# The last tiles' output sums of MoE 2 in PSUM banks of their own, one for each half of the last tile

## The chip, the cores and the metric

The kernel runs on one core of a Trainium2 chip. The metric is device time of one execution in microseconds (us); less is better. The core's engines are TensorE (PE, matmuls; its weight loads are listed apart as PEld), VectorE (DVE), ScalarE (ACT), GpSimd (POOL) and SyncE (SP, which issues the DMA transfers here). Matmuls accumulate in PSUM, which the program holds as one tile `pb` of 8 banks, each 128 partitions x 512 fp32 numbers.

## The reference

Three stages follow one another; the inputs are fp32, 2 batches x 768 positions = 1536 tokens, model width 512.

```python
attn = softmax(q @ k^T / 8 + bias, only where keep) @ v        # 2 x 8 heads x 768 x 64
x = attn, heads side by side                                   # 1536 x 512

h = x @ w_in                                                   # MoE 1: 512 -> 2048
P = a[0] + a[1]*h + a[2]*h**2 + a[3]*h**3
Q = 1 + abs(b[0])*abs(h) + abs(b[1])*h**2
y = (P / (Q + 1e-6)) @ w_out                                   # 2048 -> 512

h = y @ w2_in                                                  # MoE 2: 512 -> 1024
e = exp(h - max(h)); sm = e / (sum(e) + 1e-9)                  # along the 1024
s = h * sm
ln = (s - mean(s)) / sqrt(var(s) + 1e-6) * g_ln
out = ln @ w2_out                                              # 1024 -> 512
```

## The kernel before

**Numbers.** Every fp32 operand of a matmul is split in a high part (a cast to fp32r) and a low part (the fp32 number less the high part), and each product is three matmuls: high x high, high x low, low x high. So an operand needs a cast on ACT and a subtraction on DVE or POOL (the helper `minus`, all of whose instructions have line L99). The weights come in as words that are converted first (`w_conv`: a scaled copy into a PSUM bank on ACT, L565; bit operations in that bank on DVE or POOL and DVE, a shift at L586; a join back to SBUF on DVE, L574) and then split (`w_split`: high part on ACT, L604; low part on POOL or DVE).

**MoE 1.** The tokens go in blocks of 384, the width 2048 in slices of 128. For one block and one slice, `h_mm` makes h transposed, 128 x 384, in one bank (12 matmuls: 8 with the high weights and inputs, L634 and L636, 4 with the low inputs, L640), `e_ops` makes the fraction from it in a row of steps on ACT and DVE (L660 to L675), whose result is cast by ACT (L677, tile `g`) and subtracted by POOL (L99), and `y_mm` adds the slice's share of y into three banks (6 matmuls with the high part, L725 and L726, then 3 with the low part, L731). Of the last block the y sums of its three tiles stay in banks 5, 6 and 7 until three additions on DVE (L747) carry them to SBUF.

**MoE 2.** It goes in 12 tiles of 128 tokens (`NTILE`), called tile 0 to 11 here, in six functions:
- `p2_front`: y is transposed on PE (L791, four matmuls, "yT" below), cast to `yh` by ACT (L797) and subtracted to `yl` by DVE (L99).
- `p2_h`: the first product, in two halves of 512 columns, 12 matmuls each (L810 to L812), in two banks: 2 and 3 for even tiles, 4 and 5 for odd ones ("H2a" and "H2b" are the halves of tile 2).
- `p2_soft`: maximum (DVE, L832), exponential (ACT, L857), product with h (DVE, L838), squares (ACT, L859), an inverse root (ACT, L846 and L847, one Newton step on DVE, L850 to L853) and the normalisation (DVE, L854).
- `p2_tr`: the result is transposed on PE in two halves (L872, "lT"), each in bank 0 or 1, cast to `lh` by ACT (L880) and subtracted to `ll` by DVE (L99).
- `p2_o`: the second product, 24 matmuls over 512 columns (L894 to L896, "O0" to "O11"), all tiles in bank 7, `Val("y2")`; a copy to SBUF by ACT (L903, tile `ot`); a DMA to the output from SP (L905). Tile 11 goes in two halves of 256 columns, with two copies and two DMAs; both halves lie in the same bank, and the bank is one `Val`.

**What sets the order.** The functions above don't issue instructions, they record operations by `op(engine, duration, function, r, w, new, ...)`: values read, written, newly placed. The class `Plan` gives each a due time (`deadlines`), worked backwards along the dependencies, and then runs all engines against assumed durations (`run`): at each step, of the operations that can start now on an engine, the one due first is taken. A value made with `new` needs a free place in its pool. The PSUM pools are h (banks 0, 1), s (2, 3), p (4), y0 (5), y1 (6) and y2 (7); the values of one line take their places in the order in which they were recorded, so the weight conversions, the even tiles' first products and the attention scores follow one another in banks 2 and 3. Dependencies are by value. The argument `after` adds dependencies on whole operations; these count for the order alone.

Lines that matter, of `p2_h` and `p2_o`:

```python
for half in range(2):
    op("PE", 3.06, lambda half=half: mm(half), r=[...],
       new=[o.h[half]] if half else [o.h[0]], occ=2.76, tag="h2")

b, ot = Val("y2"), Val("wst", "ot")
parts = [op("PE", 5.52 / n + 0.3, lambda c=c: mm(c), r=[...],
            **{"w" if i else "new": [b]}, occ=5.52 / n, tag="o") for i, c in enumerate(cs)]
```

## Time and profile before

| | us |
|---|---|
| median of 3 runs (lowest to highest) | 559.95 (559.59 to 560.86) |
| the profiled execution's own time | 558.11 |
| its span in the trace | 556.3 |
| PE busy over the span | 531.8 (96%) |
| DVE busy | 446.0 (80%) |
| ACT busy | 393.0 (71%) |
| POOL busy | 182.5 (33%) |

The granted clock of TensorE is 0.999 of full speed, 2.4 GHz, over the whole execution. Attention and MoE 1 are interleaved up to about 400 us; the last first product of MoE 1 on PE ends at 390.63 us, and from 413 us on PE does MoE 2 alone. The last matmul starts at 550.15 us, and the rest of the span, some 6 us, is the last copies, their DMAs and the program's end.

How it is read: the windows show which engine is full in which stretch, the waits show what PE and DVE stood idle for, and the timelines show single instructions around the two places that the change touches, the passage from MoE 1 to MoE 2 and the last tiles. In a row of a timeline the bracket at its end is the idle time of the engine ahead of it and the instruction that ended it.

### The profile page before, as it was taken

How to read it: one execution, taken by the hardware profiler on the slowest of the kernel's cores; microseconds unless marked ns; L12 is line 12 of the kernel's file. 1: busy time of each engine (PE TensorE's matmuls, PEld its weight loads, DVE VectorE, ACT ScalarE, POOL GpSimd, SP SyncE). 2: the span in 40 equal slices, each digit the busy share in tenths (PEclk: the TensorE clock that was granted, in tenths of full speed). 3: DMA queues.
4: the chain of work that ended last, by engine and by line, in shares of the span. 5: the costliest groups of instructions: out<-in, count | busy, mean ns of one | idle time of the engine just before them, and what ended most of it. 6: DMA issues, size and time to landing. Idle time of an engine off the chain costs nothing.

```text
span 556.3 us, 8937 instructions
## 1 busy us (share of the span) xinstructions
PE 531.8 (96%) x2910; PEld 437.0 (79%) x2910; DVE 446.0 (80%) x1104; ACT 393.0 (71%) x911; POOL 182.5 (33%) x212
## 2 busy tenths in 40 slices
PE   7999999999999899999999999999999999999995
PEld 6668776877788678778788887888878788888874
DVE  4997999999999999878788999999876755455530
ACT  5688999898888878787778988898544543334330
POOL 2311665546456632122342644674510000000000
PEclk9999999999999999999999999999999999999999
DMA  7469662544354432211013322252101111000011
GB/s 252 130 201 341 195 219 86 185 135 153 104 182 154 151 96 98 73 48 48 1 38 114 133 77 75 77 180 87 57 20 38 39 38 58 20 19 20 19 39 43
DMA packets 28278, 56.24 MB, mean 101 GB/s; under 512 B 3520, under 2 KB 11968, under 8 KB 28224
## 3 DMA queue, kind: packets, MB, share of 16 engines
q1 hardware_dynamic: 28080, 55.59, 30.9%
q8 instruction: 25, 0.41, 0.3%
q14 instruction: 29, 0.24, 0.1%
q10 hardware_dynamic: 144, 0.00, 0.0%
HBM read 47.72 MB, written 7.86 MB: 100 GB/s over the span
## 4 chain that ended last, share of the span: by engine, by line
PE 55%; DVE 29%; ACT 10%; issue 4%; DMA 1%; POOL 0%; SPq 0%; ACTq 0%; DVEq 0%; POOLq 0%
PE pb L894 4%; PE pb L896 4%; PE pb L895 4%; PE pb L634 4%; PE pb L810 4%; PE pb L812 4%; PE pb L811 4%; PE pb L640 4%; PE pb L731 3%; PE pb L636 3%; PE pb L725 3%; DVE t L667 3%; PE pb L459 3%; DVE wst L574 3%; PE pb L726 3%
## 5 line engine op out<-in xcount | busy, mean ns | idle before, releaser
L99 POOL TENSOR_TENSOR g<-t,g 128x384 fp32r<-128x384 f32 x64 | 69.2, 1082 | 103.9 <-ACT g L677 91.7
L634 PE MATMUL pb<-x,w 128*128 128x384 f32 x256 | 89.3, 349 | 1.8 <-DVE t L667 1.8
L636 PE MATMUL pb<-x,w 128*128 128x384 f32 x256 | 86.1, 336 | 0.0
L725 PE MATMUL pb<-w,g 128*128 128x512 f32 x192 | 77.5, 404 | 4.2 <-ACT g L677 4.2
L726 PE MATMUL pb<-w,g 128*128 128x512 f32 x192 | 75.6, 394 | 0.5 <-POOL w L99 0.5
L99 POOL TENSOR_TENSOR w<-wst,w 128x512 fp32r<-128x512 f32 x42 | 57.2, 1364 | 42.7 <-ACT w L604 38.8
L640 PE MATMUL pb<-x,w 128*128 128x384 f32 x256 | 58.0, 347 | 0.1
L731 PE MATMUL pb<-w,g 128*128 128x512 f32 x192 | 57.7, 409 | 0.2 <-POOL g L99 0.2
L634 PEld LDWEIGHTS pb<-x,w 128*128 128x128 f32 x256 | 48.1, 188 | 8.6 <-DVE t L667 4.4
L471 ACT ACTIVATE e<-e,st 128x256 f32<-128x256 f32 (+1 forms) x96 | 46.3, 486 | 6.4 <-DVE st L464 6.4
L640 PEld LDWEIGHTS pb<-x,w 128*128 128x128 f32 x256 | 44.5, 188 | 7.1 <-issue 3.1
L636 PEld LDWEIGHTS pb<-x,w 128*128 128x128 f32 x256 | 48.1, 188 | 1.5
L725 PEld LDWEIGHTS pb<-w,g 128*128 128x128 f32 x192 | 36.0, 187 | 14.4 <-ACT g L677 7.3
L660 ACT ACTIVATE t<-pb,coef 128x384 f32<-128x384 f32 x64 | 42.7, 668 | 6.1 <-PE pb L640 6.1
L482 POOL TENSOR_SCALAR e<-e,st 128x256 f32<-128x256 f32 (+1 forms) x58 | 28.0, 495 | 54.4 <-DVE st L477 48.4
L669 ACT ACTIVATE t<-t,coef 128x384 f32<-128x384 f32 x64 | 39.6, 618 | 6.8 <-DVE t L667 6.6
L662 DVE TENSOR_TENSOR t<-t,pb 128x384 f32<-128x384 f32 x64 | 35.2, 549 | 11.1 <-ACT t L663 6.5
L677 ACT CAST g<-t 128x384 fp32r<-128x384 f32 x64 | 32.8, 512 | 16.0 <-DVE t L675 15.3
L880 ACT CAST lh<-pb 128x512 fp32r<-128x512 f32 x24 | 13.9, 592 | 42.5 <-PE pb L872 42.5
L459 PE MATMUL pb<-qk 64*128 64x256 f32 (+3 forms) x192 | 41.3, 393 | 2.7 <-DVE st L464 1.0
L667 DVE SCALAR_TENSOR_TENSOR t<-pb,coef,t 128x384 f32<-128x384 f32 x64 | 39.2, 613 | 5.2 <-ACT pb L666 4.8
L671 DVE SCALAR_TENSOR_TENSOR t<-t,t 128x384 f32<-128x384 f32 x64 | 40.6, 634 | 1.3 <-ACT t L670 1.3
(113 smaller groups left out, 1293.2 us busy)
## 6 DMA issues: line engine op xcount, KB each, us to landing
wst<-in_w_in SPq DMA_DIRECT2D x24, 512.0 KB, 4.0
wst<-in_w_out SPq DMA_DIRECT2D x24, 512.0 KB, 3.7
qk<-in_qkv SPq DMA_DIRECT2D x40, 256.0 KB, 2.7
v<-in_qkv SPq DMA_DIRECT2D x40, 128.0 KB, 2.5
y_d<-y SPq DMA_DIRECT2D x12, 256.0 KB, 2.5
y<-y_d SPq DMA_DIRECT2D x12, 256.0 KB, 2.6
out<-wst SPq DMA_DIRECT2D x11, 256.0 KB, 2.0
qk<-in_qkv SPq DMA_DIRECT2D x8, 192.0 KB, 3.7
```

The costliest lines, as they stand in the source:

```text
L99: eng.tensor_tensor(out=out, in0=a, in1=hi.bitcast(F32), op=ALU.subtract)
L459: pe.matmul(out=score(h), lhsT=a[r, h * 128:(h + 1) * 128], rhs=a[r, 256:256 + w], start=True, stop=True)
L471: act.activation(out=e[:, h, 0:w], in_=e[:, h, 0:w], func=AF.Exp, scale=-1.0, bias=st[:, h:h + 1], accum_out=st[:, 2 + 2 * h:3 + 2 * h])
L634: pe.matmul(out=pb[:, g.h.slot, 0:n], lhsT=wt[wh.slot][:, cs[p]], rhs=xt[x[p][0].slot][:, 0:n], start=(p == 0), stop=False)
L636: pe.matmul(out=pb[:, g.h.slot, 0:n], lhsT=wt[wl.slot][:, cs[p]], rhs=xt[x[p][0].slot][:, 0:n], start=False, stop=False)
L640: pe.matmul(out=pb[:, g.h.slot, 0:n], lhsT=wt[wh.slot][:, cs[p]], rhs=xt[x[p][1].slot][:, 0:n], start=False, stop=(p == 3))
L660: op("ACT", 0.2 + 0.46 * k, lambda: act.activation(out=T(g.c), in_=h(), func=AF.Identity, scale=coef[:, 3:4], bias=coef[:, 2:3]), r=[g.h], ...
L667: op("DVE", 0.2 + 0.41 * k, lambda: stt_(out=T(g.a), in0=h(), scalar=coef[:, 5:6], in1=T(g.b), op0=ALU.mult, op1=ALU.add), r=[g.h, g.b], n ...
L671: op("DVE", 0.15 + 0.41 * k, lambda: stt_(out=T(g.a), in0=T(g.a), scalar=1.0 + 1e-6, in1=T(g.b), op0=ALU.add, op1=ALU.mult), r=[g.b], w=[g ...
L725: pe.matmul(out=pb[:, y[i].slot, :], lhsT=gt[g.gh.slot][:, c], rhs=wt[wh.slot], start=g.first, stop=False)
L726: pe.matmul(out=pb[:, y[i].slot, :], lhsT=gt[g.gh.slot][:, c], rhs=wt[wl.slot], start=False, stop=False)
L731: pe.matmul(out=pb[:, y[i].slot, :], lhsT=gt[g.gl.slot][:, c], rhs=wt[wh.slot], start=False, stop=g.last)
```

## The change

**In `p2_o`.** The sums of tile 10 go to bank 6 (`Val("y1")`) instead of bank 7. The halves of tile 11 are two values: the first in bank 7, the second in bank 2 (`Val("s")`); each copy reads only its own. Tiles 0 to 9 stay in bank 7.

**In `p2_h`.** The first half of a tile's first product now claims both banks of the tile at once, where each half claimed its own before. Both halves depend, through `after`, on all the conversions' scaled copies recorded so far but the last two (`scaled`, filled in `w_conv`).

The diff also brings two further switches, `ROOT` and `EARLY`, which are off (`False` and empty) and leave the program as it is, but for a small SBUF tile `cf` that nothing uses. No instruction is added or removed: each engine executes the same operations, in another order from about 298 us of the old trace on.

```diff
+ROOT, EARLY, ENDS = False, (), True
...
-    nconv, nlo = [0], [0]
+    nconv, nlo, scaled = [0], [0], []
...
-        op("ACT", 0.63, scale, r=[st], new=[bank] + list(new), lead=WLEAD, tag="wsc")
+        scaled.append(op("ACT", 0.63, scale, r=[st], new=[bank] + list(new), lead=WLEAD, tag="wsc"))
...
             op("PE", 3.06, lambda half=half: mm(half), r=[o.yh, o.yl] + [v for m in range(4) for v in W["i2", m, half]],
-               new=[o.h[half]] if half else [o.h[0]], occ=2.76, tag="h2")
+               **{"w" if half else "new": o.h[1:] if half else o.h}, occ=2.76, after=scaled[:-2], tag="h2")
...
-        b, ot = Val("y2"), Val("wst", "ot")
-
-        def mm(c):
+        ot = Val("wst", "ot")
+        bs = [Val("y2")] if n == 1 else [Val("y2"), Val("s" if ENDS else "y2")]
+        if ENDS and o.k == NTILE - 2:
+            bs = [Val("y1")]
+        if n == 2 and not ENDS:
+            bs[1] = bs[0]
+
+        def mm(c, b):
...
-        parts = [op("PE", 5.52 / n + 0.3, lambda c=c: mm(c), r=[o.lh, o.ll] + [v for f in range(8) for v in W["o2", f]],
-                    **{"w" if i else "new": [b]}, occ=5.52 / n, tag="o") for i, c in enumerate(cs)]
         for i, c in enumerate(cs):
-            op("ACT", 0.59 / n, lambda c=c: act.copy(wst[ot.slot].bitcast(F32)[:, c], pb[:, b.slot, c]), r=[b],
+            b = bs[i]
+            op("PE", 5.52 / n + 0.3, lambda c=c, b=b: mm(c, b), r=[o.lh, o.ll] + [v for f in range(8) for v in W["o2", f]],
+               **{"w" if i and b is bs[0] else "new": [b]}, occ=5.52 / n, tag="o")
+        for i, c in enumerate(cs):
+            b = bs[i]
+            op("ACT", 0.59 / n, lambda c=c, b=b: act.copy(wst[ot.slot].bitcast(F32)[:, c], pb[:, b.slot, c]), r=[b],
                **{"w" if i else "new": [ot]}, tag="ot")
```

The order moves at three places. In the rows below `L` is the line (the second file has other numbers), the tile written stands left of the arrow and the tiles read right of it; `pb` is PSUM, `w` a weight, `wst` a staging tile that also holds MoE 2's exponentials, and the number behind a name's underline only tells the buffer.

**PE where MoE 1 ends.** Before, from the last two matmuls of a y sum (high part of `g0`) on; then come the first product's first matmuls of tile 0 (`yh0`):

```order
L725 MATMUL pb_89<-w56_148,g0_169 128x512
L726 MATMUL pb_89<-w57_149,g0_169 128x512
L810 MATMUL pb_89<-w1_93,yh0_2936 128x512
L811 MATMUL pb_89<-w0_92,yh0_2936 128x512
L812 MATMUL pb_89<-w1_93,yl0_2938 128x512
```

Now, from the same two matmuls on (L725, L726 and L731 have become L767, L768 and L773; L791 is L833, L810 is L852):

```order
L767 MATMUL pb_89<-w56_148,g0_169 128x512
L768 MATMUL pb_89<-w57_149,g0_169 128x512
L833 MATMUL pb_89<-ident_65,y2_191 128x128 x4
L773 MATMUL pb_89<-w56_148,g1_170 128x512 x3
L767 MATMUL pb_89<-w58_150,g2_171 128x512
L768 MATMUL pb_89<-w59_151,g2_171 128x512
L767 MATMUL pb_89<-w58_150,g2_171 128x512
L768 MATMUL pb_89<-w59_151,g2_171 128x512
L767 MATMUL pb_89<-w58_150,g2_171 128x512
L768 MATMUL pb_89<-w59_151,g2_171 128x512
L852 MATMUL pb_89<-w1_93,yh0_2937 128x512
```

The first transpose of y and the next y sum (high part of `g2`) now stand ahead of tile 0's first product, which starts one y sum later. On ACT, correspondingly, the cast `yh0` now stands right ahead of the cast to that `g2`; before, it stood nine instructions further ahead, in front of the cast to `g0` as well. Behind these rows PE did H0b, yT1, H1a, both lT of tile 0, yT2, H1b, H2a, H2b, with three y sums among the first of them; now it does H0b, yT1, H1a, yT2, H1b, H2a, lT0a, H2b, lT0b, with the y sums all ahead of H1a.

**DVE around tile 0's normalisation.** Before, from the last Newton step on (L854 is the normalisation, L586 and L574 the last weight conversion, in bank 2, L747 the three y sums, L832 the maximum of tile 1):

```order
L853 TENSOR_SCALAR st20_2940<-st20_2940 128x1
L854 TENSOR_SCALAR wst0_156<-wst0_156,st20_2940 128x1024
L586 SCALAR_TENSOR_TENSOR pb_89<-pb_89,wst3_159 128x512
L747 TENSOR_TENSOR y1_190<-pb_89,y1_190 128x512
L747 TENSOR_TENSOR y3_192<-pb_89,y3_192 128x512
L747 TENSOR_TENSOR y0_189<-pb_89,y0_189 128x512
L574 SCALAR_TENSOR_TENSOR wst3_159<-wst3_159,pb_89 128x512
L99 TENSOR_TENSOR yl0_2938<-pb_89,yh0_2936 128x512
L99 TENSOR_TENSOR ll0_2945<-pb_89,lh0_2943 128x512
L832 TENSOR_REDUCE st21_2941<-pb_89 128x1
```

Now (L896 is the normalisation, L618 and L606 the conversion, L789 the y sums, L874 the maximum of tile 1):

```order
L789 TENSOR_TENSOR y3_192<-pb_89,y3_192 128x512
L789 TENSOR_TENSOR y0_189<-pb_89,y0_189 128x512
L789 TENSOR_TENSOR y1_190<-pb_89,y1_190 128x512
L885 TENSOR_SCALAR st20_2941<-st20_2941 128x1
L892 TENSOR_TENSOR st20_2941<-st20_2941 128x1
L893 SCALAR_TENSOR_TENSOR st20_2941<-st20_2941 128x1
L894 SCALAR_TENSOR_TENSOR st20_2941<-st20_2941 128x1
L895 TENSOR_SCALAR st20_2941<-st20_2941 128x1
L896 TENSOR_SCALAR wst0_156<-wst0_156,st20_2941 128x1024
L618 SCALAR_TENSOR_TENSOR pb_89<-pb_89,wst3_159 128x512
L103 TENSOR_TENSOR yl0_2939<-pb_89,yh0_2937 128x512
L606 SCALAR_TENSOR_TENSOR wst3_159<-wst3_159,pb_89 128x512
L874 TENSOR_REDUCE st21_2942<-pb_89 128x1
```

The y sums moved ahead of the normalisation, the low part of the third y (`yl0`) between the two steps of the conversion, and `ll0` behind the maximum of tile 1.

**PE between the last tiles' second products.** Before, from the last three matmuls of O8 to the first three of O9 (each in bank 7):

```order
L894 MATMUL pb<-w_123,lh_2943 128x512
L895 MATMUL pb<-w_122,lh_2943 128x512
L896 MATMUL pb<-w_123,ll_2945 128x512
L872 MATMUL pb<-ident,wst_156 128x128 [waits DVE_49]
L872 MATMUL pb<-ident,wst_156 128x128 x3
L894 MATMUL pb<-w_109,lh_2944 128x512 [waits Activation_49]
L895 MATMUL pb<-w_111,lh_2944 128x512
L896 MATMUL pb<-w_109,ll_2946 128x512
```

Now, the same two products, each still in bank 7:

```order
L941 MATMUL pb<-w_123,lh_2944 128x512
L942 MATMUL pb<-w_122,lh_2944 128x512
L943 MATMUL pb<-w_123,ll_2946 128x512
L941 MATMUL pb<-w_109,lh_2945 128x512 [waits Activation_49]
L942 MATMUL pb<-w_111,lh_2945 128x512
L943 MATMUL pb<-w_109,ll_2947 128x512
```

The transposes that stood between O8 and O9 now stand ahead of O8, so O9 follows O8 at once. What stands between a second product and the one ahead of it, before: for O1 to O8 at least one half of a first product, for O9 one lT, for O10 two lT, for O11 nothing. Now: for O2 and O6 one yT, for O9 nothing, for O10 (in bank 6) two lT, for O11 nothing (its first half lies in bank 7, last used by O9), for the others at least one half of a first product.

## Rows read from the trace of the kernel before

**Rows 1.** The page: busy time and share of the span, by engine.

```profile
PE 531.8 (96%) x2910; PEld 437.0 (79%) x2910; DVE 446.0 (80%) x1104; ACT 393.0 (71%) x911; POOL 182.5 (33%) x212
```

**Rows 2.** Windows: length, then busy time of PE, PEld, DVE, ACT, POOL, clock.

```profile
300.00:340.00 40.00, 38.89 (x192) 34.59 (x193) 38.56 (x69) 34.60 (x69) 19.23 (x19) 1.00 0.34 112
340.00:380.00 40.00, 37.12 (x180) 31.67 (x179) 39.10 (x71) 34.14 (x68) 24.55 (x22) 1.00 0.42 139
...
460.00:500.00 40.00, 40.00 (x196) 33.42 (x195) 19.79 (x48) 14.83 (x30) 0.00 (x0) 1.00 0.08 27
```

**Rows 3.** What PE waited for, 296 to 392 us: total us, times, longest.

```profile
PE pb L725 <- ACT g L677: 2.8, 4, 1.0
PE pb L634 <- DVE t L667: 1.2, 2, 0.8
```

**Rows 4.** What DVE waited for, 296 to 392 us.

```profile
DVE t L667 <- ACT pb L666: 1.0, 2, 0.6
DVE t L662 <- ACT t L660: 0.7, 1, 0.7
```

**Rows 5.** Timeline of PE where MoE 2 begins: start, us, operation, [idle ahead <-releaser].

```profile
392.02 0.39 PE L810 MATMUL pb<-w,yh 128*128 128x512 f32 x1
...
394.75 0.84 PE L731 MATMUL pb<-w,g 128*128 128x512 f32 x3
395.44 0.39 PE L810 MATMUL pb<-w,yh 128*128 128x512 f32 x1
...
398.15 0.39 PE L725 MATMUL pb<-w,g 128*128 128x512 f32 x1
...
408.69 1.09 PE L872 MATMUL pb<-ident,wst 128*128 128x128 f32 x8 [0.77 <-DVE wst L854]
409.89 0.66 PE L791 MATMUL pb<-ident,y 128*128 128x128 f32 x4
410.48 0.50 PE L810 MATMUL pb<-w,yh 128*128 128x512 f32 x1
...
413.33 0.39 PE L810 MATMUL pb<-w,yh 128*128 128x512 f32 x1
```

**Rows 6.** Timeline of DVE in the same stretch.

```profile
398.36 1.23 DVE L832 TENSOR_REDUCE st<-pb 128x1 f32<-128x1024 f32 x1 [0.16 <-PE pb L812]
...
407.82 0.81 DVE L854 TENSOR_SCALAR wst<-wst,st 128x1024 f32<-128x1024 f32 x1
408.55 0.69 DVE L586 SCALAR_TENSOR_TENSOR pb<-pb,wst 128x512 int32<-128x512 int32 x1
409.15 1.88 DVE L747 TENSOR_TENSOR y<-pb,y 128x512 f32<-128x512 f32 x3
410.94 0.68 DVE L574 SCALAR_TENSOR_TENSOR wst<-wst,pb 128x512 int32<-128x512 int32 x1
411.54 0.69 DVE L99 TENSOR_TENSOR yl<-pb,yh 128x512 fp32r<-128x512 f32 x1
```

**Rows 7.** Timeline of ACT in the same stretch.

```profile
392.59 0.53 ACT L670 ACTIVATE t<-t 128x384 f32<-128x384 f32 x1
393.10 0.51 ACT L677 CAST g<-t 128x384 fp32r<-128x384 f32 x1
...
400.83 0.58 ACT L797 CAST yh<-pb 128x512 fp32r<-128x512 f32 x1
```

**Rows 8.** Timeline of PE in MoE 2: the transposes at 432 us, O9, the last tile.

```profile
432.45 0.66 PE L872 MATMUL pb<-ident,wst 128*128 128x128 f32 x4 [0.80 <-DVE ll L99]
...
530.75 0.60 PE L872 MATMUL pb<-ident,wst 128*128 128x128 f32 x4
531.60 0.50 PE L894 MATMUL pb<-w,lh 128*128 128x512 f32 x1 [0.24 <-ACT wst L903]
...
544.50 0.39 PE L894 MATMUL pb<-w,lh 128*128 128x256 f32 x1 [0.68 <-ACT wst L903]
...
550.15 0.28 PE L896 MATMUL pb<-w,ll 128*128 128x256 f32 x1
```

**Rows 9.** Timeline of ACT at the end.

```profile
543.87 0.59 ACT L903 COPY wst<-pb 128x512 f32<-128x512 f32 x1 [4.89 <-PE pb L896]
550.51 0.65 ACT L903 COPY wst<-pb 128x256 f32<-128x256 f32 x2 [6.06 <-PE pb L896]
```

**Rows 10.** Timeline of SP's queue at the end.

```profile
550.91 0.81 SPq L905 DMA_DIRECT2D out<-wst  x2
```

More of the change, by code (lines that the diff above doesn't have):

```diff
@@ L417, in bias_pair, with root_log, root_end @@
             act.mul(bt[h], dz, -8.0 * SLOPE[h])
+    vcf = Val()
+    cf = const.tile([128, 4], F32, name="cf")
+    def root_log():
+        act.activation(out=cf[:, 1:2], in_=cf[:, 0:1], func=AF.Ln)
+        act.activation(out=cf[:, 1:2], in_=cf[:, 1:2], func=AF.Exp, scale=0.5)
+    def root_end():
+        dve.reciprocal(out=cf[:, 2:3], in_=cf[:, 1:2])
+        dve.scalar_tensor_tensor(out=cf[:, 1:2], in0=cf[:, 0:1], scalar=cf[:, 2:3], in1=cf[:, 1:2], op0=ALU.mult, op1=ALU.add)
+        dve.tensor_scalar(out=cf[:, 1:2], in0=cf[:, 1:2], scalar1=0.5, scalar2=None, op0=ALU.mult)
+        dve.reciprocal(out=cf[:, 2:3], in_=cf[:, 1:2])
+        dve.tensor_tensor(out=cf[:, 3:4], in0=cf[:, 2:3], in1=coef[:, 4:5], op=ALU.mult)
     op("POOL", 0.9, bias_iota, new=vt0)
@@ L423, in record @@
         op("ACT", 0.75, lambda p=p: bias_pair(p), r=vt0, w=[vbias[p]], tag="bias")
+    if ROOT:
+        op("DVE", 0.15, lambda: dve.tensor_scalar(out=cf[:, 0:1], in0=coef[:, 5:6], scalar1=1e-30, scalar2=None, op0=ALU.max), w=[vcf], tag="cf")
+        op("ACT", 0.5, root_log, w=[vcf], tag="cf")
+        op("DVE", 0.75, root_end, w=[vcf], tag="cf")
     class U:
@@ L436, in uop, with aside, qk_of, v_of @@
         uops.append(op(*a, **k))
+    def aside(u):
+        return u.j in EARLY and u.k % 2 == 1
+    def qk_of(u):
+        return yt[u.qk.slot] if aside(u) else qkt[u.qk.slot]
+    def v_of(u):
+        return tt[u.v.slot] if aside(u) else vt[u.v.slot]
     def u_load(u):
-        u.qk, u.v = Val("qk"), Val("v")
+        u.qk, u.v = (Val("y", "qk0"), Val("t", "v0")) if aside(u) else (Val("qk"), Val("v"))
         w = 256 + u.w
-        uop("SP", 2.4, lambda: sync.dma_start(out=qkt[u.qk.slot][:, 0:w], in_=qkv[u.t, u.p, :, 0:w]), occ=0.4,
+        uop("SP", 2.4, lambda: sync.dma_start(out=qk_of(u)[:, 0:w], in_=qkv[u.t, u.p, :, 0:w]), occ=0.4,
             new=[u.qk], move=0.8, tag="ld")
-        uop("SP", 2.4, lambda: sync.dma_start(out=vt[u.v.slot][:, 0:u.w], in_=qkv[u.t, u.p, :, w:w + u.w]), occ=0.4,
+        uop("SP", 2.4, lambda: sync.dma_start(out=v_of(u)[:, 0:u.w], in_=qkv[u.t, u.p, :, w:w + u.w]), occ=0.4,
             new=[u.v], move=0.4, tag="ld")
@@ L455, in qk @@
         def qk():
-            a = qkt[u.qk.slot]
+            a = qk_of(u)
             for h in range(2):
@@ L508, in pv @@
                     v0 = k * 128 + h * 64
-                    pe.matmul(out=pb[h * 64:(h + 1) * 64, u.xp.slot, 0:128], lhsT=vt[u.v.slot][:, v0:v0 + 64],
+                    pe.matmul(out=pb[h * 64:(h + 1) * 64, u.xp.slot, 0:128], lhsT=v_of(u)[:, v0:v0 + 64],
                               rhs=ptt[:, c:c + 128], start=(k == 0), stop=(k == n - 1))
@@ L659, in e_ops @@
         stt_ = dve.scalar_tensor_tensor
-        op("ACT", 0.2 + 0.46 * k, lambda: act.activation(out=T(g.c), in_=h(), func=AF.Identity, scale=coef[:, 3:4], bias=coef[:, 2:3]),
-           r=[g.h], new=[g.c], tag="c")
-        op("DVE", 0.14 + 0.41 * k, lambda: dve.tensor_tensor(out=T(g.c), in0=T(g.c), in1=h(), op=ALU.mult), r=[g.h], w=[g.c], tag="ch")
-        op("ACT", 0.15 + 0.42 * k, lambda: act.activation(out=T(g.b), in_=h(), func=AF.Abs, scale=coef[:, 4:5]), r=[g.h], new=[g.b], tag="abs")
```

24 lines of the change are left out of this document (19 added, 5 removed).

## The prediction, made before the changed kernel was run

> **What bounds the kernel now.** First the busy times of the page: PE has 96% of the span, so only what PE waits for can be won, some 24 us in all, and most of that lies at the start and behind the last matmul [rows 1]. Then the windows: between 300 and 380 us PE and DVE are both nearly full (PE 38.89 and 37.12 of 40, DVE 38.56 and 39.10), while in MoE 2 PE has 40.00 of 40 and DVE half of that [rows 2]. So towards the end of MoE 1 two engines bound the kernel together, and from about 413 us on PE alone does: there only an idle gap of PE, or what follows its last matmul, is worth anything. Then the waits: from 296 to 392 us PE waited 4.0 us, for casts and for DVE [rows 3], and DVE waited for ACT, 1.7 us in the two rows shown [rows 4]. Last the timelines, for the gaps in MoE 2. There are four: 0.77 us ahead of tile 0's transposes [rows 5], 0.80 at 432.45, 0.24 ahead of O9 and 0.68 ahead of O11 [rows 8]. The last two are what the bank costs: O11's first matmul waits until ACT has copied O10 out of bank 7 (copy from 543.87, 0.59 us long [rows 9], next matmul at 544.50). As a loss of PE such a wait is more than its idle time, since matmuls otherwise start while the one ahead is still draining (0.23 us apart at a busy time of 0.39): I put 0.86 on O11's gap from the cadence of 0.23, and 0.40 on O9's, where one lT lies between (531.60 less 530.75 is 0.85, where four transposes take 0.44).
>
> **The change part by part.**
>
> *The last tile's halves.* Before, both copies start only behind the second half, at 550.51, 0.65 us for the two [rows 9], and SP issues two DMAs, 0.81 us for the two, so the last is issued near 551.32 [rows 10]. Now the first half's copy and DMA lie some 2.8 us earlier, under the second half's matmuls. What is left behind the last matmul is one copy and one issue: the last issue moves from 551.32 to 550.91. **-0.41 us.** All of it is on the path that sets the end.
>
> *Tile 10 in bank 6.* O10 no longer shares a bank with O11, whose first half writes bank 7, free since O9's copy. So the gap of 0.68 ahead of O11 goes: **-0.86.** What is late next there is the cast and subtraction of tile 11's transposes, and O10's 5.5 us cover them.
>
> *O9 right behind O8.* Both still lie in bank 7, and the lT that stood between them now stands ahead. This is the very case of O10 and O11 before: **+0.86**, with the 0.40 that the lT left uncovered before taken off: O9 before cost 0.40 [rows 8]. Net +0.46.
>
> *O2 behind O1, O6 behind O5.* Same bank, with one yT of 0.44 between: each costs what O9 did with one lT, 0.40, so **+0.80**.
>
> *Transposes.* Both lT of tile 2 again stand in a pair behind another, as at 432.45 (loss 0.95 there); the second one's wait for DVE may be a little longer, as the DVE's row of steps is denser here: **+0.1**, between 0 and 0.4.
>
> *The seam.* With no shift of MoE 1, PE ends its last first product at 390.63 and the first y sum at 392.02 [rows 5]. Now: yT0 (0.44) and a low part (0.69) to 393.15, then the next y sum, which needs its cast. ACT ends the step ahead of that cast at 393.12 [rows 7], then does `yh0` (0.58, as at 400.83) and only then the cast (0.51): 394.2 instead of 393.6. The sum starts at 394.2, a gap of 1.0 us where there was none. It takes 1.37, H0a 2.73 (392.02 to 394.75), the low part 0.69, H0b 2.72: H0b ends at 401.7 instead of 398.15. From there DVE's maximum to the end of the normalisation took 10.27 us (398.36 to 408.63 [rows 6]); the steps in this chain wait for ACT more than for DVE, so I keep it: 412.1. Then comes the last conversion: shift 0.69, `yl0` 0.69, join 0.68, each starting some 0.08 ahead of the one before's end: 413.9. H2a needs bank 2, which this conversion holds. PE by itself would be there at 401.7 + 10.3 (two y sums with their low parts 4.1, H1a and H1b 5.45, two yT 0.7) = 412.0, so it stands for 1.9 us. Before, H2a started at 413.33 with both lT of tile 0 done (0.87, still to do now): 413.9 - 413.33 + 0.87 = **+1.4**. Against it stands that in the last 30 us of MoE 1 DVE's work on the fractions stands earlier: one subtraction (0.69) and one conversion step (0.68) are moved behind the last fractions. As DVE is nearly full there [rows 2], the last first product may end that much earlier; I take half: **-0.7**, between -2 (the two steps and what they release of PE's waits [rows 3]) and +1.2 (the other steps of the conversions, moved later by 2 to 6 us of DVE's work, stop a product that needs their weights, a wait as long as the longest here, 1.0, or somewhat more).
>
> No transfer is added; SP's and POOL's orders keep the same work, and SP's last transfers have nothing queued ahead of them.
>
> **The sum.** -0.41 - 0.86 + 0.46 + 0.80 + 0.1 + 1.4 - 0.7 = **+0.8**. The sum is made on the profiled execution, 558.11 (span 556.3 and 1.8 around it), that is 558.9; on the median of the runs, 559.95, which lies 1.84 above that execution, it gives **560.7**. What the title speaks of, the banks and the halves, makes -0.41 - 0.86 + 0.46 + 0.80 = 0.0 by itself; the sign comes from the seam. Change and no change can be told apart at about 0.2%, 1.1 us.
>
> **The rivals.**
>
> *The banks give what they are meant to, and nothing is paid back* (559.95 - 0.41 - 0.86 = **558.7**). For it: both gaps are plain in the trace and their causes go. Against it: O9 is moved into the same case as O11 was. It comes out so if the seam is neutral and O2, O6 and O9 lose no more in sum than O9 did before. The Trainium skill, "Perfetto Trace Analysis", in its section on matmuls, says that independent groups of matmuls should rotate through different PSUM banks, so that one group's evacuation overlaps the next group's matmuls. The row of O11 bears it out (a stand of 0.68 us behind a copy of 0.59), but the rule would have O8 and O9 rotated as well, which this change doesn't do: by that rule -0.86 for the last pair stands, and so does +0.86 for the earlier one.
>
> *MoE 1 gains.* The end of MoE 1 has 4.0 us of PE's waits [rows 3]; if the new order frees 2 of them, the -0.7 above becomes -2.0 and the time is 560.7 - 1.3 = **559.4**. Against it: DVE's own waits there are only some 2 us [rows 4], so a fuller DVE can't give much more.
>
> *The seam loses (slower).* Tile 0's first product is started a y sum later, and everything of MoE 2's start follows it: H0, its normalisation, the conversion in bank 2, H2a. If MoE 1's end doesn't come earlier, the -0.7 is gone, and if `yl0` and the join wait for PE's transposes as well, or the conversions that were moved later stop a first product for 1.0 us, it is 560.7 + 0.7 + 1.0 = **562.4**. It decides from H0b's end: at 401.0 or earlier it is my sum, at 402 or later this one.
>
> *The change doesn't do what it says*: if the second half's copy still starts behind something else, or the program's end waits for the earlier DMA's landing all the same, the tail gives 0 and the sum is +1.2: **561.1**.
>
> **How the numbers follow.** My sum 0.40 (559.6 to 561.8 on its own); the banks alone 0.15; MoE 1 gains 0.12; the seam loses 0.27; no effect at the tail 0.06. The likeliest is 560.7. The range leaves out a part of the banks' case, that with a gain in MoE 1 on top, and the seam's upper end with a stop of more than 1 us: **558.5 to 562.8**. Faster by over 0.2% (under 558.8): two thirds of the first rival (0.10), a third of the second (0.04) and a tail of my sum (0.03), 0.17. Slower by over 0.2% (over 561.1): nearly all of the seam's case (0.25), three tenths of my sum (0.12) and a part of the last case (0.02), 0.39. Between: 0.44.
>
> **What would show it.** In the profile after, the copies of the halves should stand apart, the first near 2.8 us ahead of the second, with one DMA issue behind the last. O11's first matmul should follow O10's last without a gap; O9's should have a gap of about 0.7 that is ended by the copy, O2's and O6's about 0.2. At the seam: a gap of about 1 us ahead of the y sum before H0a, and a gap ahead of H2a that is ended by DVE's join (L606). I am wrong if the last first product of MoE 1 ends more than 1.5 us from 390.6, or if H2a doesn't wait.

## The result, and the profile after

The changed kernel takes 563.12 us (median of 6 runs, 562.20 to 564.36), the kernel before 559.83 in the same comparison: a ratio of 1.0063, with a 95% interval of 1.0044 to 1.0081, so 2.5 to 4.5 us slower. Forecast were 560.7, at most 562.8.

The two profiled executions can't be subtracted as they are: 563.39 less 558.11 is 5.3 us, more than the runs say. Nearly half of it comes from the start, where the programs are the same: the first 318 us took 2.5 us longer in the profiled execution after. It was 2.1 us behind by 12 us and 3.5 by 30 us (2.6 at 297 us); a part of it is that the granted clock of TensorE fell to half near 26 us. The windows of that execution (length, busy time of PE, PEld, DVE, ACT, POOL, then the clock):

```profile
24.00:26.00 2.00, 2.00 (x14) 1.68 (x12) 1.93 (x10) 1.99 (x9) 0.41 (x1) 0.67 0.33 80
26.00:28.00 2.00, 2.00 (x9) 1.12 (x8) 1.61 (x3) 0.51 (x3) 0.87 (x1) 0.50 0.33 117
```

So all traces are compared from one landmark on: the first matmul of the 49th of MoE 1's 64 first products, the last product up to which PE's order agrees (those of DVE, ACT and POOL part some 10 us ahead of it). It stands at 318.63 us before and at 321.10 after, in the timelines of PE:

```profile
318.63 0.45 PE L634 MATMUL pb<-x,w 128*128 128x384 f32 x1
```
```profile
321.10 0.33 PE L666 MATMUL pb<-x,w 128*128 128x384 f32 x1
```

In the executions told of below it lies between 317.90 and 321.10, whichever the order behind it, so it tells of the execution and not of the change. From it, in us (the first column is read at the start of the matmul behind that product, the last from the span, which the profile gives to 0.1 us):

| | last first product of MoE 1 ends | O0 begins | last matmul ends | span ends |
|---|---|---|---|---|
| before | 72.00 | 100.50 | 231.80 | 237.67 |
| after | 72.78 | 102.45 | 235.21 | 240.50 |
| difference | +0.78 | +1.95 | +3.41 | +2.83 |

The change costs 2.83 us in this pair, inside the interval of the runs. About 0.8 is lost by the end of MoE 1, 1.2 in the passage to MoE 2, 1.5 in MoE 2, and 0.6 comes back behind the last matmul. What PE waited for in the stretch, from 290 to 557 us of the trace after (total, times, longest; answering to [rows 3, 5, 8]):

```profile
PE pb L767 <- ACT g L719: 2.6, 7, 0.7
PE pb L666 <- DVE t L709: 1.9, 2, 1.6
PE pb L941 <- ACT wst L953: 1.8, 3, 0.8
PE pb L852 <- DVE wst L606: 1.1, 1, 1.1
PE pb L914 <- DVE ll L103: 0.8, 1, 0.8
```

The third row is the change's own subject: the waits for the copy out of an output bank were 0.9 us in two places and are now 1.8 in three. The fourth is new: H2a waits for the join of the last weight conversion. The wait for the normalisation ahead of tile 0's transposes is gone. In the timeline of PE these places look so (first the passage, answering to [rows 5], then O2, which had no stand before, and O9):

```profile
393.88 0.40 PE L767 MATMUL pb<-w,g 128*128 128x512 f32 x1
...
397.21 0.51 PE L767 MATMUL pb<-w,g 128*128 128x512 f32 x1 [0.66 <-ACT g L719]
...
398.74 0.47 PE L852 MATMUL pb<-w,yh 128*128 128x512 f32 x1
...
416.76 0.47 PE L852 MATMUL pb<-w,yh 128*128 128x512 f32 x1 [1.12 <-DVE wst L606]
...
457.12 0.50 PE L941 MATMUL pb<-w,lh 128*128 128x512 f32 x1 [0.85 <-ACT wst L953]
...
538.50 0.50 PE L941 MATMUL pb<-w,lh 128*128 128x512 f32 x1 [0.72 <-ACT wst L953]
```

ACT shows two causes: `yh` ahead of the cast to `g` that PE stands for at 397.21, and the squares of another tile (L901) ahead of O1's copy, which O2 stands for at 457.12. At the end the copies stand apart, as the change means it [rows 9]:

```profile
396.19 0.57 ACT L839 CAST yh<-pb 128x512 fp32r<-128x512 f32 x1
396.65 0.51 ACT L719 CAST g<-t 128x384 fp32r<-128x384 f32 x1
...
455.36 1.12 ACT L901 ACTIVATE pb<-wst,st 128x1024 f32<-128x1024 f32 x1 [2.40 <-DVE st L881]
456.42 0.19 ACT L901 ACTIVATION_READ_ACCUMULATOR pb<-wst,st 128x1 f32 x1
456.51 0.56 ACT L953 COPY wst<-pb 128x512 f32<-128x512 f32 x1
...
550.69 0.59 ACT L953 COPY wst<-pb 128x512 f32<-128x512 f32 x1 [4.82 <-PE pb L943]
553.57 0.37 ACT L953 COPY wst<-pb 128x256 f32<-128x256 f32 x1 [2.29 <-PE pb L943]
556.35 0.37 ACT L953 COPY wst<-pb 128x256 f32<-128x256 f32 x1 [2.41 <-PE pb L943]
```

And DVE shows what H2a waits for: normalisation, shift, `yl`, join, in a row without a gap [rows 6]:

```profile
414.01 0.81 DVE L896 TENSOR_SCALAR wst<-wst,st 128x1024 f32<-128x1024 f32 x1
414.74 0.69 DVE L618 SCALAR_TENSOR_TENSOR pb<-pb,wst 128x512 int32<-128x512 int32 x1
415.33 0.68 DVE L103 TENSOR_TENSOR yl<-pb,yh 128x512 fp32r<-128x512 f32 x1
415.93 0.68 DVE L606 SCALAR_TENSOR_TENSOR wst<-wst,pb 128x512 int32<-128x512 int32 x1
```

### The profile page after: what moved, and what is told of

Its sections match the earlier page's. It is cut to its first block, busy times and chain, and to the rows that moved or that the text cites. A ratio compares the mean times of both kernels' runs of the same rounds, so it can differ in the third digit from the quotient of the medians.

```text
span 561.6 us, 8945 instructions
## 1 busy us (share of the span) xinstructions
PE 536.8 (96%) x2910; PEld 439.5 (78%) x2910; DVE 447.9 (80%) x1104; ACT 392.7 (70%) x911; POOL 181.6 (32%) x212
## 4 chain that ended last, share of the span: by engine, by line
PE 55%; DVE 28%; ACT 11%; issue 4%; DMA 1%; POOL 0%; SPq 0%; ACTq 0%; DVEq 0%
PE pb L666 4%; PE pb L672 4%; PE pb L767 4%; PE pb L668 4%; PE pb L491 4%; PE pb L773 4%; PE pb L768 4%; PE pb L852 3%; PE pb L854 3%; PE pb L853 3%; PE pb L941 3%; PE pb L943 3%; PE pb L942 3%; DVE wst L606 3%; PE pb L541 3%
## 5 line engine op out<-in xcount | busy, mean ns | idle before, releaser
L767 PE MATMUL pb<-w,g 128*128 128x512 f32 x192 | 78.0, 406 | 4.0 <-ACT g L719 4.0
L768 PE MATMUL pb<-w,g 128*128 128x512 f32 x192 | 75.6, 394 | 0.5 <-POOL w L103 0.5
L773 PE MATMUL pb<-w,g 128*128 128x512 f32 x192 | 57.9, 410 | 0.2 <-POOL g L103 0.2
L767 PEld LDWEIGHTS pb<-w,g 128*128 128x128 f32 x192 | 36.0, 187 | 15.3 <-ACT g L719 8.3
L717 DVE SCALAR_TENSOR_TENSOR t<-t,coef,t 128x384 f32<-128x384 f32 x64 | 41.3, 646 | 1.3
L941 PE MATMUL pb<-w,lh 128*128 128x512 f32 (+1 forms) x104 | 40.0, 384 | 1.8 <-ACT wst L953 1.8
```

Of the source, the lines that this page charges most:

```text
L717: op("DVE", 0.2 + 0.43 * k, lambda: stt_(out=T(g.c), in0=T(g.c), scalar=coef[:, 0:1], in1=T(g.b), op0=ALU.add, op1=ALU.mult), r=[g.b], w=[ ...
L767: pe.matmul(out=pb[:, y[i].slot, :], lhsT=gt[g.gh.slot][:, c], rhs=wt[wh.slot], start=g.first, stop=False)
L768: pe.matmul(out=pb[:, y[i].slot, :], lhsT=gt[g.gh.slot][:, c], rhs=wt[wl.slot], start=False, stop=False)
L773: pe.matmul(out=pb[:, y[i].slot, :], lhsT=gt[g.gl.slot][:, c], rhs=wt[wh.slot], start=False, stop=g.last)
L941: pe.matmul(out=pb[:, b.slot, c], lhsT=lh[:, f, :], rhs=wh[:, c], start=(f == 0), stop=False)
```

## The experiments

All are told with the ratio to the kernel before on the same chip (95% interval in brackets) and with the four times from the landmark. A "stand" is a place where PE stood. A figure in a bracket of a row is its idle time alone. From start to start, from the matmul ahead to the next one, H2a's stand measures 1.51 us, O9's and O2's 1.12, O6's 0.51 in the changed kernel; less the ordinary step (0.23 behind a matmul, 0.03 behind transposes) PE loses 1.3, 0.9, 1.1 and 0.5 us there. The texts on record take 0.1 for that step.

**Which half of the change loses?** The banks alone, and the order alone. With `p2_h` recorded as before, the planner gives the old order back, instruction by instruction; with the last tiles' sums in one bank again but `p2_h` new, it gives the changed kernel's. So the two halves of the change come apart cleanly: `p2_o` moves banks and no instruction, `p2_h` moves instructions and no bank of an output.

Banks alone, from the changed kernel:

```diff
-               **{"w" if half else "new": o.h[1:] if half else o.h}, occ=2.76, after=scaled[:-2], tag="h2")
+               new=[o.h[half]] if half else [o.h[0]], occ=2.76, tag="h2")
```

> The new banks of tile 10 and of the last half, with the first product recorded as before; the order of every engine is then that of the kernel before, instruction by instruction, and only the banks differ. Theory A (the banks gain what they free, the loss comes from the new order): O11 follows O10 without the 0.86 us, the last copy and issue come 0.41 us earlier, so about 1.3 us faster than before, 558.5 against 559.8. Theory B (the separate halves or banks cost something themselves, in the copies or the last DMAs): 560 or more.

Measured: 0.9978 (0.9958 to 0.9997), about 1.2 us faster than before. From the landmark: 71.96, 100.46, 230.66, 235.93. Up to O0 it is the kernel before to 0.04 us; the last matmul is 1.14 us earlier, and behind it 5.27 us are left instead of 5.87. O11's stand is gone, O9's is left, as the waits of PE from 500 to 550 us say in a single row:

```profile
PE pb L941 <- ACT wst L953: 0.2, 1, 0.2
```

The order alone:

```diff
-ROOT, EARLY, ENDS = False, (), True
+ROOT, EARLY, ENDS = False, (), False
```

> The first product recorded in the new way, the last tiles' sums all in one bank as before; the order of every engine is that of the changed kernel, and only the banks of the last two tiles differ from it. Theory A: the loss of the order stands alone, the changed kernel's 563.1 plus 0.86 (O11 behind O10) plus 0.41 (both copies behind the last matmul), about 564.4. Theory B: 561 or less, since what costs is the banks.

Measured: 1.0091 (1.0065 to 1.0117), 5.1 us slower than before. From the landmark: 72.78, 102.50, 236.26, 242.24. Up to O0 it is the changed kernel to 0.05 us, from there it loses 1.00 us by O11's stand and 0.69 behind the last matmul, where the copies wait together again:

```profile
555.90 0.65 ACT L953 COPY wst<-pb 128x256 f32<-128x256 f32 x2 [6.06 <-PE pb L943]
```

Theory A holds in both: the banks gain at least what was forecast for them (1.27 us; 1.74 at the span's end by the landmark in either order, 1.2 by the runs in the old one), and the order loses some 4.6 us by the landmark.

**Which half of the new recording loses?** The claim of both banks, and the dependency on the conversions.

```diff
-               **{"w" if half else "new": o.h[1:] if half else o.h}, occ=2.76, after=scaled[:-2], tag="h2")
+               **{"w" if half else "new": o.h[1:] if half else o.h}, occ=2.76, tag="h2")
```

> The changed kernel without the dependency on the conversions' scaled copies: both banks of a first product are claimed at once, nothing else of that function. In its order tile 0's first product stands again where it stood before, second products stand twice with one transpose of y between them, and O9 has its one lT again. If the claim alone makes the loss: 563 or more. If the dependency makes the passage from MoE 1 late and the claim only costs the two pairs: -1.3 for the banks, +1.4 for the pairs as the changed kernel's trace shows them (1.0 and 0.4), about 560.

Measured: 1.0026 (1.0006 to 1.0046), 1.5 us slower, where about as fast as before was expected. From the landmark: 71.98, 94.69, 232.94, 238.49. MoE 1 ends exactly as before, so the claim alone doesn't touch it. In MoE 2 two pairs with one yT between them are there, in this order O2 and O3, O6 and O7, with the losses of the changed kernel's two (1.1 and 0.5), and one stand that I had not put in, 1.64 us ahead of tile 0's transposes, which wait longer for the normalisation than the 0.77 of before:

```profile
410.56 0.66 PE L914 MATMUL pb<-ident,wst 128*128 128x128 f32 x4 [1.64 <-DVE wst L896]
```

Then the dependency alone:

```diff
-               **{"w" if half else "new": o.h[1:] if half else o.h}, occ=2.76, after=scaled[:-2], tag="h2")
+               new=[o.h[half]] if half else [o.h[0]], occ=2.76, after=scaled[:-2], tag="h2")
```

> The changed kernel with each half claiming its own bank as before, but with the dependency on the conversions' scaled copies. In its order tile 0's first product stands one y sum later as in the changed kernel, no two second products stand with one transpose between them, O9 stands right behind O8. If the dependency makes the loss by the late passage: -1.3 for the banks, +0.6 for O9 (1.0 less the 0.4 before), +2 to +2.5 for the passage, about 561.5. If the passage costs nothing: 559.2.

In this order a conversion and a half of a first product come into the same bank, so a part of the numbers is overwritten; the operations are the same ones. Measured: 1.0142 (1.0113 to 1.0171), 8 us slower, much more than expected. The last first product of MoE 1 ends at 72.80 from the landmark, as in the changed kernel: it is the dependency that makes the loss of 0.8 there. The rest is a fault of this order alone, a stand of 5.29 us in one place, behind which the matmuls go at half the rate for a while:

```profile
427.96 1.33 PE L914 MATMUL pb<-ident,wst 128*128 128x128 f32 x5 [5.29 <-DVE wst L896]
```

So the run answers for MoE 1 and not for the passage. It also shows why the two edits come together: with the dependency, one claim for both banks is what keeps the conversions out of them.

**The pairs, and H2a.** Two runs leave the changed kernel's order as it is and only choose another bank when the instructions are written: O2, O6 and O9 in bank 3, or the last conversion in bank 0.

```diff
+        def at(b, i):
+            return {(2, 0): 3, (6, 0): 3, (9, 0): 3}.get((o.k, i), b.slot)
...
-                pe.matmul(out=pb[:, b.slot, c], lhsT=lh[:, f, :], rhs=wh[:, c], start=(f == 0), stop=False)
+                pe.matmul(out=pb[:, at(b, i), c], lhsT=lh[:, f, :], rhs=wh[:, c], start=(f == 0), stop=False)
```

> The changed kernel, the order of every engine unchanged, with O2, O6 and O9 in bank 3 instead of bank 7, so that each of the three pairs of second products lies in two banks. Theory A (the three stands of PE are the shared bank's alone): they measured 1.10, 0.48 and 1.12 us in the changed kernel, of which 0.1 each is an ordinary step, so 2.4 us faster than it, about 0.9 slower than before. Theory C (a wait of another engine, such as the cast of the transposes, stands right behind the bank's): under 1 us faster than the changed kernel, over 2.3 slower than before.

Measured: 1.0004 (0.9980 to 1.0028). From the landmark: 72.83, 102.53, 232.67, 238.05, so the last matmul ends 2.54 us earlier than in the changed kernel. All three stands are gone and nothing stands in their place; the waits for ACT's copies are no longer among PE's waits:

```profile
PE pb L767 <- ACT g L719: 2.7, 7, 0.7
PE pb L666 <- DVE t L709: 1.6, 1, 1.6
PE pb L852 <- DVE wst L606: 1.1, 1, 1.1
```

The conversion:

```diff
-            return w[:, :, 0], w[:, :, 1], pbi[:, bank.slot, :]
+            return w[:, :, 0], w[:, :, 1], pbi[:, 0 if last else bank.slot, :]
...
-        zero = nconv[0] in ZS
+        zero, last = nconv[0] in ZS, nconv[0] == 47
```

> The changed kernel, the order unchanged, with the last weight conversion in bank 0 instead of bank 2. Theory A (tile 2's first product waits for the conversion that holds its bank): H2a, which stood for 1.51 us, now waits only for the low part of its y, which DVE has ready 0.6 us ahead of the conversion's last step; 0.8 to 1.1 us faster than the changed kernel, about 2.4 slower than before. Theory C (DVE's row of steps sets that passage): H2a comes earlier, but tile 0's transposes or the first second product stand for the time that it won, no gain.

Measured: 1.0032 (1.0014 to 1.0050), 1.8 us slower than before. From the landmark: 72.81, 101.23, 234.03, 239.56: O0 begins 1.22 us earlier than in the changed kernel, and the last matmul ends 1.18 earlier. H2a's stand is gone: its first matmul starts at 414.93, the ordinary 0.23 behind the one ahead. A stop of 0.1 is left at its third matmul, which needs `yl`; it is too small for a bracket in the timeline of PE (the one behind it starts 0.34 later, where 0.23 is ordinary):

```profile
415.15 0.39 PE L853 MATMUL pb<-w,yh 128*128 128x512 f32 x1
415.38 0.50 PE L854 MATMUL pb<-w,yl 128*128 128x512 f32 x1
415.72 0.40 PE L852 MATMUL pb<-w,yh 128*128 128x512 f32 x1
```

Theory A again in both. From the end of MoE 1 to O0 it is 28.42 us here, 29.67 in the changed kernel and 28.50 before, so this one bank is all that the passage lost. Then both together:

> The changed kernel with both repairs of banks together: O2, O6, O9 in bank 3 and the last conversion in bank 0, the order unchanged. If the two losses are separate, the gains add: 2.5 and 1.2 us under the changed kernel, so 0.3 to 0.9 us faster than before, and still about 1 us slower than the kernel before with the same banks (which was 0.40% faster than before): that rest is the end of MoE 1. If they overlap: no faster than before.

Measured: 0.9968 (0.9952 to 0.9985), 1.8 us faster than before, more than the 0.3 to 0.9 expected; by the landmark 72.81, 101.25, 231.39, 236.82, that is 0.85 us faster. The gains add: 2.54 and 1.18 are 3.72, and it is 3.82 less at the last matmul than in the changed kernel.

**The end of MoE 1.** The stretch from the landmark to the end of the last first product is 72.78 to 72.83 us in every such execution with the dependency, 71.96 to 72.03 in every one without it. To see whether DVE makes the difference, five weight conversions (42 to 46) do their DVE steps on 32 of 512 columns, in both orders, one execution each; these weights are then not converted, and the output is another one. `few()` cuts the columns; the shift is shown, the other DVE steps are cut in the same way:

```diff
-        zero = nconv[0] in ZS
+        zero, less = nconv[0] in ZS, 42 <= nconv[0] <= 46
...
         def shift():
-            w0, w1, a = words()
+            w0, w1, a = few()
```

> The changed kernel, its order unchanged, with the DVE steps of weight conversions 42 to 46 (the last but one of 48) on 32 of 512 columns only: those weights are not converted, so the output is another one; it leaves out some 7 us of DVE's work between 364 and 398 us. Read between the start of the 48th slice's product, where both orders are still the same, and the end of the last first product, 72.78 us in the changed kernel. Theory D (the new order loses at the end of MoE 1 since conversions are put off to where DVE is full): PE's stands of the last 20 us go and the stretch comes to 70.5 to 71.5. Theory E (the order of PE and ACT loses by itself): 72.3 or more.

> The same omission in the kernel before, in its own order: the control; its stretch was 71.99 us, with the first transposes of y (0.5 us) in it, which the changed kernel does later. Theory D: DVE is full here too, so it gains as well, but less than the changed kernel, since fewer of these steps lie in its last 20 us: 71.0 to 71.5, so that the difference between the two orders falls from +0.8 to between -0.5 and +0.2. Theory E: both gain alike and +0.8 stays.

Measured: 70.06 in the new order, 2.72 us less; 71.15 in the old one, 0.85 us less. The difference between the orders goes from +0.78 to -1.09, further than either number that I had written. Of the waits of PE between 374 and 394 us the changed kernel has

```profile
PE pb L666 <- DVE t L709: 1.6, 1, 1.6
PE pb L767 <- ACT g L719: 1.2, 3, 0.7
```

of which the first belongs to a stand from 373.1 to 374.69 us; without the conversions only this is left between 374 and 393 us:

```profile
PE pb L770 <- ACT g L722: 0.7, 1, 0.7
```

and that one is at the passage. The stand of 1.6 us is not gone with them, though. It only lies ahead of this window:

```profile
372.53 0.44 PE L669 MATMUL pb<-x,w 128*128 128x384 f32 x1 [1.56 <-DVE t L712]
```

What goes are the stands behind it. So theory D holds in its main point: with the same steps shortened, the new order gains three times as much as the old one, hence its end of MoE 1 is set by DVE's work. Its reason, that conversions are put off to where DVE is full, the traces don't bear out as it stands. The joins of the last eight conversions do come 1.6 to 6.7 us later from the landmark. But the windows of the last 17 to 19 us show DVE as full before (16.54 of 16.80, the first row) as after (18.89 of 19.20):

```profile
373.80:390.60 16.80, 16.44 (x83) 14.31 (x82) 16.54 (x31) 13.99 (x28) 8.18 (x10) 1.00 0.31 106
374.70:393.90 19.20, 17.99 (x85) 15.01 (x86) 18.89 (x32) 14.92 (x30) 11.12 (x12) 1.00 0.32 112
```

And by the timelines of DVE the conversions are as many: 27 steps between the landmark and the end of MoE 1 in either order, 7 of them in the last 20 us. In the new order two steps are moved out of the stretch behind its end, but two others come into it from ahead of the landmark.

What differs in the traces is how long DVE's steps take. Both orders leave DVE idle for 2.1 to 2.2 us of the stretch, and the new one has three steps fewer (122 for 125). But the fraction's steps between SBUF tiles (L713, L715, L717) take longer when they start while POOL is inside an instruction. The longest takes 1.58 us, where the median of its line is 0.62; the cast to `g` behind it starts at 383.89, and PE stands for that cast (DVE, POOL, PE):

```profile
382.27 1.58 DVE L717 SCALAR_TENSOR_TENSOR t<-t,coef,t 128x384 f32<-128x384 f32 x1
...
382.15 1.29 POOL L103 TENSOR_TENSOR w<-wst,w 128x512 fp32r<-128x512 f32 x1 [0.24 <-ACT w L636]
...
384.45 0.50 PE L767 MATMUL pb<-w,g 128*128 128x512 f32 x1 [0.66 <-ACT g L719]
```

Over the stretch DVE's long steps together take 2.4 us more than the medians of their lines in every execution of the new order with whole conversions, 1.0 us in every such one of the old order. The 1.5 us between them are about what the end of MoE 1 lost. That is read from the traces alone; no run moves these POOL instructions, so as a cause it is not shown.

**The passage's first stand.** One exchange on ACT: the cast to `g` that PE waits for ahead of `yh`.

```diff
-                o.fn()
+                if o.tag == "yh" and self.swap is None:
+                    self.swap = o
+                else:
+                    o.fn()
+                    if o.tag == "gh" and self.swap:
+                        self.swap.fn()
+                        self.swap = False
```

> The changed kernel with one pair of instructions on ACT exchanged: the cast to g for the next y sum ahead of tile 0's yh, everything else in its place. Theory A (the passage starts late by that cast): the stand of 0.66 us ahead of the y sum falls to about 0.2, tile 0's first product and what follows come 0.45 us earlier, so about 0.45 us faster than the changed kernel, 0.55% slower than before. Theory C (DVE's steps decide the passage): the stand goes, but H2a waits longer by as much, under 0.2 us.

Measured: 1.0059 (1.0037 to 1.0082), the changed kernel's ratio; by the landmark 72.82, 102.94, 235.74, 241.25, half a microsecond slower than it. Both theories miss. The stand falls from 0.66 to 0.18 us, but the next one opens at once, ahead of tile 0's first product (timeline of PE):

```profile
395.13 0.51 PE L774 MATMUL pb<-w,g 128*128 128x512 f32 x1 [0.18 <-ACT g L726]
...
397.56 0.47 PE L859 MATMUL pb<-w,yh 128*128 128x512 f32 x1 [0.75 <-DVE wst L613]
```

L613 is the join of the last conversion but one, which holds a bank of that product. On DVE it stands behind `yl`, and `yl` waits for the `yh` that was put later:

```profile
395.60 0.69 DVE L103 TENSOR_TENSOR yl<-pb,yh 128x512 fp32r<-128x512 f32 x1 [0.33 <-ACT yh L846]
...
396.73 0.68 DVE L613 SCALAR_TENSOR_TENSOR wst<-wst,pb 128x512 int32<-128x512 int32 x1
```

So tile 0's first product starts at 78.11 from the landmark instead of 77.64, and H2a 0.47 us later as well (96.13 instead of 95.66). The cast's place on ACT was a stand, but not the one that set the passage.

**A version that beats both.** The old order, the changed kernel's banks, and O9 in bank 3:

```diff
+        def at(i):
+            return {(NTILE - 3, 0): 3, (NTILE - 2, 0): 6, (NTILE - 1, 1): 2}.get((o.k, i), b.slot)
```

> The kernel before, in its own order, with the changed kernel's banks for the last two tiles and O9 in bank 3: all three last second products in banks of their own. 0.3 to 0.4 us under the run with the banks alone, which was 0.22% faster than before; so about 1.5 us faster than before, 0.27%. If O9's stand was the copy's place on ACT and not its bank, nothing more than 0.22%.

Measured: 0.9960 (0.9942 to 0.9979), 2.2 us faster than before, where the changed kernel is 3.5 slower (0.40% and 0.63%). The last matmul ends at 230.27 from the landmark, 0.39 earlier than with the banks alone: O9's stand was its bank. The span ends at 235.90, against 235.93, since behind the last matmul 5.63 us are left here and 5.27 there; with two banks for the halves this rest was between 5.27 and 5.63 in all executions, with one bank 5.87 to 5.98. Last, the same with tile 2's first transposes in bank 7:

```diff
+            def at(b, x=x):
+                return 7 if (o.k, x) == (2, 0) else b.slot
```

> As the run before it, and the first transposes of tile 2's result in bank 7 instead of a bank from which DVE still subtracts. They stood for 0.80 us (1.04 with what a step costs); that goes if the bank alone held them, so about 2.5 us faster than before, 0.45%. If the next matmuls, which need the same casts, stand instead, no gain over the run before.

Measured: 0.9969 (0.9951 to 0.9987), no gain that the runs can tell; the last matmul ends 0.20 us earlier by the landmark. The stand of 0.80 is gone, and 0.24 us of it come back at the next product, which waits for `yh`, with a stop at its third matmul besides (434.98 instead of 434.82):

```profile
433.41 0.60 PE L875 MATMUL pb<-ident,wst 128*128 128x128 f32 x4
434.25 0.50 PE L810 MATMUL pb<-w,yh 128*128 128x512 f32 x1 [0.24 <-ACT yh L797]
434.59 0.40 PE L811 MATMUL pb<-w,yh 128*128 128x512 f32 x1
434.98 0.50 PE L812 MATMUL pb<-w,yl 128*128 128x512 f32 x1
```

So the bank was one cause there and ACT's and DVE's row of casts a second one right behind it.

## Why the prediction was wrong

By its own steps, each against what the traces show from the landmark:

- *The last tile's halves*, -0.41: right in kind, a little more in size. Behind the last matmul 0.58 us less are left (0.60 with the banks alone).
- *Tile 10 in bank 6*, -0.86: right in kind. With the banks alone the last matmul ends 1.14 us earlier, with the order alone the shared bank costs 1.00.
- *O9 right behind O8*, +0.86 for the pair: right. The stand measures 1.12 from start to start, of which 0.23 is the ordinary step, so 0.89; with O9 in bank 3 in the same order only that step is left.
- *O2 behind O1, O6 behind O5*, +0.40 each: mis-sized. O6 lost 0.5, O2 1.1. The step that failed here is "each costs what O9 did with one lT": at O9 ACT had nothing else to do, at O1's end it was in the squares of tile 5 (455.36 to 456.6), and the copy waited for them. I had looked at the bank and at PE, and not at what is queued ahead of the copy on ACT.
- *Transposes*, +0.1: nothing came of it. The second lT of tile 2 stands for 0.79 us (waits of PE above), 0.80 before.
- *The seam*, +1.4 without a shift of MoE 1: right in its mechanism and near in size. The y sum stood 0.66 us for its cast (forecast 1.0), H2a 1.5 for the conversion in its bank (forecast 1.9), and from the last first product to O0 the changed kernel takes 1.17 us more. With that conversion in another bank the 1.17 are gone. On the clock of before the conversion's join ends at 414.14 us (416.61 after, less the landmarks' 2.47), forecast 413.9. Of the cast this can't be said: it stood, but with its stand taken away nothing was gained.
- *The end of MoE 1*, -0.7: this is the step that failed. It came out at +0.78, and the changed kernel has 0.5 us of transposes less in that stretch, so the loss is 1.3. The step was to take DVE's time as shorter by "one subtraction and one conversion step", moved behind the last fractions. The subtraction is moved out, but for the two conversion steps that go out two others come in from ahead of the landmark, which was not counted: 27 before, 27 now. And it took every step of DVE at the same price in either order, where the long ones took 1.5 us more in the new one. The conversions that move later were put into the range only; that DVE's work sets the end is what the short conversions show (2.72 us of the new order's stretch, 0.85 of the old one's). Which of its steps make the 1.3 us stays open.

With the measured sizes in their places the sum is +0.8 for MoE 1, +1.2 for the passage, +1.5 for MoE 2 and -0.6 behind it: +2.8. The forecast of 0.8 was 1.5 too low in the first, 1.0 in the third. Of the rivals, "the seam loses" is the one that came about, at 562.4: MoE 1's end did not come earlier, and H0b ended at 402.5 on the clock of before (404.98 after, brought to it by the landmarks' 2.47), past the point that it named. Its price is near by luck in part: no first product stopped for its weights in the traces, and O2's stand, which makes up for it, was in no rival. Neither sign of being wrong that the prediction names showed: on the clock of before the last first product ended at 391.4, 0.8 us from 390.6, and H2a did wait. That the title's banks would gain, the first rival, is true of the banks by themselves, and was hidden under an order that has nothing to do with them. The rule of rotating the banks, for which the prediction names the Trainium skill ("Perfetto Trace Analysis", section "Matmuls"), held for O8 and O9 as for O10 and O11: in bank 3 O9 stands no more and starts 0.23 us behind O8's last matmul.

What isn't settled: the medians of the runs put the changed kernel 3.3 us above the one before, the traces 2.8; the interval covers both. And why the all-apart version is 1.8 us faster than before by its runs and 0.85 by its trace was not looked into further than that the starts of single executions differ by up to 3 us.

## What to carry to other kernels

A change of banks in a kernel whose order a planner makes is two changes: write the banks in without letting the planner see them, and the order stays; here, with one bank more, that turned a loss of 0.6% into a gain of 0.4%. When a change moves work along an engine that is full, count what comes into the stretch as well as what leaves it, and look whether the steps that stay are still as short. And where two groups share a bank, the cost is not the copy but the copy and whatever stands ahead of it on its engine.

## What the runs showed of the hardware

The start of an execution varies more than the change weighs: the same instructions reach the landmark between 317.90 and 321.10 us, and the granted clock of TensorE went to 0.50, 1.2 GHz, for about 3 us near 26 us in one execution, where PE had been busy for 1.16 of the 2 us from 22 to 24; in the profiled execution of before PE had the same pause (1.22 of 2 us, from 20 to 22), and the clock stayed at 1.00. A long stand has the same price: in the run with the dependency alone PE stood for 5.29 us, and the clock was at half over the stand's end and the 4 us after it, though PE worked again from 427.96 on (windows as above):

```profile
424.00:426.00 2.00, 0.00 (x0) 0.00 (x0) 1.65 (x4) 1.97 (x6) 0.00 (x0) 0.89 0.30 109
426.00:428.00 2.00, 0.04 (x1) 0.04 (x1) 1.86 (x7) 2.00 (x4) 0.00 (x0) 0.50 0.00 0
428.00:430.00 2.00, 2.00 (x9) 2.00 (x10) 1.93 (x5) 0.62 (x2) 0.00 (x0) 0.50 0.00 0
430.00:432.00 2.00, 2.00 (x6) 1.52 (x6) 1.44 (x4) 1.09 (x2) 0.00 (x0) 0.50 0.00 0
432.00:434.00 2.00, 2.00 (x10) 1.60 (x9) 1.39 (x6) 0.93 (x5) 0.00 (x0) 0.90 0.00 0
```

The stands of 1 to 2 us in the other traces left the clock at 1.00.

A late landmark does not need that fall of the clock: with the last conversion apart it lies at 320.54 us, and the clock was at 1.00 up to there.

Some of DVE's steps end only behind POOL's. In the two stretches behind the landmark, 22 of DVE's steps with two inputs in SBUF and the output there (L713, L715 and L717, or L671, L673 and L675 before) start while POOL is inside an instruction, and each of them ends at least 0.39 us behind the end of that instruction: the 1.58 us from 382.27 end at 383.85, POOL's 1.29 us from 382.15 at 383.44. The medians of these lines are 0.55 to 0.62 us.
